# Block sums stored a group later, token blocks loaded a group sooner, and copied reciprocals in the attention

## The chip, the cores and the metric

One core of a Trainium2 chip runs the whole program. TensorE (PE) multiplies matrices, PEld is its weight load, VectorE (DVE), ScalarE (ACT) and GpSimd (POOL) work on tiles, and SyncE (SP) issues DMAs from one queue, in order. The metric is the device time of one execution in microseconds, as a median of runs. "Granted clock" is the share of TensorE's full clock that the throttle gave.

## What is computed

Attention between tokens and a small state for 8 batches, then eight experts of equal capacity, then a gated layer (silu) over all 4608 tokens:

```python
def reference(**kwargs):
    attn_out = _attn_ref(x, state)            # 8 batches, 8 heads, 512 tokens, 32 states, 64 wide
    x = attn_out.transpose(0, 2, 1, 3).reshape(B * S, H * D)   # 4608 x 512
    x = _moe_ref(x=x, **moe_kwargs)           # 8 experts of 576 tokens, 512 -> 1024 -> 512
    return _moe2_ref(x=x, **moe2_kwargs)      # 512 -> 1536 -> 512

def _moe2_ref(x, w_gate, w_val, w_out):
    g = x @ w_gate
    silu = g * (1.0 / (1.0 + np.exp(-g)))
    val = x @ w_val
    return (silu * val @ w_out).astype(np.float32)

def _attn_ref(x, state):
    scores = scale * np.matmul(x, state.transpose(0, 1, 3, 2))
    ...                                       # softmax over the states: a
    xread = np.matmul(a, state)
    scores2 = scale * np.matmul(state, x.transpose(0, 1, 3, 2))
    ...                                       # softmax over the tokens: a2
    sread = np.matmul(a2, x)
    return np.concatenate([xread, sread], axis=2).astype(np.float32)
```

## The kernel before

Four parts follow each other. The attention runs batch by batch up to some 150 us; the experts' tokens are then selected; eight experts run up to 649 us; the gated layer, here called the passes, fills the rest. In all of them a scheduler places the instructions on the engines' queues in list order, as far as the buffers of the tile pools allow; each engine then executes its own queue in order.

*Attention.* Float32 products are made from high and low halves: `turn_x` transposes tokens on PE, ACT casts the high half xTh (L235), DVE subtracts to get the low half xTl (L236). `prep_state` does the same for the state (SBh on ACT L198, SBl on DVE L199, four pieces of each). `scores` multiplies them into z (L249 to L251); `center` transposes z on DVE and subtracts the maximum on POOL (zc, L261). `xread` multiplies the exponentials e1h and e1l (e1l on POOL, L286) with the state into px, ACT copies px to xu (L321), DVE makes the reciprocals rd (L325, L326), weights the gate's columns with them (xw, L327), and POOL weights the values with the same rd (xm, L333). This happens twice in each batch, for two halves of its tokens.

*Passes.* The gated layer is a seven-product scheme in blocks. `hidden_units` lists two passes, of nine groups each (eight experts' tokens and the remainder group E in the middle), and of three units in each group; unit (n, jj) here is the jj-th of the n-th group of the first pass. A unit is 84 matmuls on PE (L1076) into four banks. ACT copies the first bank (s1, L1106), DVE adds the others up (u2 L1109, u3 L1112, cs L1115, L1121, L1124), ACT and DVE apply the gate (m, L1083 and L1084), and SP stores m (L1127). PE uses the banks of the unit before the last again, so it waits when s, u or cs are late.

Between a unit's steps the next group's operands are made: `y_load` (L955) loads a block of tokens, `y_sums` lets POOL form four sums of it (L902 to L905, tiles tt, a ring of six), `keep` stores them for the second pass (L878), and `y_combo` splits each operand into a high half (ACT, L864) and a low half (DVE, L865), in a ring of tiles yb. An operand comes straight from the loaded block (raw: 1, 2, 3) or from a sum (6, 7, 5, 4). Pairs of weight blocks go the same way (L890 to L893, w). `convert` turns a block of weights as loaded (raw64, one buffer, L171) into float32 with ACT (L179) and DVE (L181, L182, L184), and SP stores it (v_d, L185), and then loads the next block into that one buffer.

## Time and profile before

| | us |
|---|---|
| median of 3 runs | 1452.44 (1451.69 to 1453.4) |
| profiled execution | 1450.2 |
| its span | 1448.6 |
| PE busy in it | 1368.3 (94%) |
| DVE busy | 1072.4 (74%) |
| ACT busy | 571.5 (39%) |
| POOL busy | 455.8 (31%) |

The profiled execution is one run of its own, and all durations below are from it; 1.6 us of it lie outside the span. Busy shares are means over the four parts. Idle time of PE is put down to what ended it: the row of a matmul has it in brackets, with the engine and the tile that came last.

### The profile page before, as it was taken

How to read it: one execution, taken by the hardware profiler on the slowest of the kernel's cores; microseconds unless marked ns; L12 is line 12 of the kernel's file. 1: busy time of each engine (PE TensorE's matmuls, PEld its weight loads, DVE VectorE, ACT ScalarE, POOL GpSimd, SP SyncE). 2: the span in 40 equal slices, each digit the busy share in tenths (PEclk: the TensorE clock that was granted, in tenths of full speed). 3: DMA queues.
4: the chain of work that ended last, by engine and by line, in shares of the span. 5: the costliest groups of instructions: out<-in, count | busy, mean ns of one | idle time of the engine just before them, and what ended most of it. 6: DMA issues, size and time to landing. Idle time of an engine off the chain costs nothing.

```text
span 1448.6 us, 28968 instructions
## 1 busy us (share of the span) xinstructions
PE 1368.3 (94%) x11440; PEld 1323.6 (91%) x11441; DVE 1072.4 (74%) x2052; ACT 571.5 (39%) x1124; POOL 455.8 (31%) x392
## 2 busy tenths in 40 slices
PE   6998388999999999999999999999999999999996
PEld 5777278999999999999899999999999999999996
DVE  5899768876877765558776766777756588998982
ACT  6875123332333334345233333433323264444441
POOL 4775211100110110333442300112311007778872
PEclk9999699999999999999999999999999999999999
DMA  7542324444446355427674563766675384434431
GB/s 132 127 116 85 116 70 175 155 150 155 131 137 197 125 156 176 162 79 269 209 278 171 189 204 114 250 228 233 227 274 183 114 308 154 146 121 159 158 102 44
DMA packets 122823, 238.36 MB, mean 165 GB/s; under 512 B 47808, under 2 KB 57024, under 8 KB 116288
## 3 DMA queue, kind: packets, MB, share of 16 engines
q1 hardware_dynamic: 109008, 207.65, 42.8%
q0 software_dynamic: 6112, 19.93, 4.1%
q10 hardware_dynamic: 7568, 8.95, 2.0%
q8 instruction: 89, 1.46, 0.4%
q14 instruction: 46, 0.38, 0.1%
HBM read 153.65 MB, written 82.84 MB: 163 GB/s over the span
## 4 chain that ended last, share of the span: by engine, by line
PE 75%; issue 5%; DMA 3%; DVE 3%; ACT 1%; POOL 0%; SPq 0%; POOLq 0%; DVEq 0%; ACTq 0%
PE b L1076 47%; PE h L821 13%; PE y L840 4%; PE y L836 4%; PE y L837 4%; PE bt L800 1%; DVE yb L865 1%; DMA raw<-in_moe_w_val_dram 1%; DMA raw<-y_d 1%; DMA xg<-xm_d,idx 1%; DMA raw<-v_d 0%; DMA v_d<-tt 0%; PE acc L476 0%; PE acc L565 0%; DVE cs L1115 0%
## 5 line engine op out<-in xcount | busy, mean ns | idle before, releaser
L1076 PE MATMUL b<-yb,w 128*128 128x256 f32 x4320 | 519.7, 283 | 11.1 <-DVE cs L1115 6.9
L1076 PEld LDWEIGHTS b<-yb,w 128*128 128x128 f32 x4320 | 517.0, 191 | 13.6 <-DVE cs L1115 8.1
L1076 PE MATMUL b<-w,yb 128*128 128x256 f32 x2160 | 257.5, 282 | 0.0
L1076 PEld LDWEIGHTS b<-w,yb 128*128 128x128 f32 x2160 | 257.4, 189 | 0.0
L821 PE MATMUL h<-xh,w 128*128 128x288 f32 (+1 forms) x1024 | 212.0, 298 | 1.3 <-ACT xh L805 0.7
L865 DVE TENSOR_TENSOR yb<-tt,yb 128x512 fp32r<-128x512 f32 x164 | 153.4, 950 | 18.4 <-ACT yb L864 17.3
L821 PEld LDWEIGHTS h<-xh,w 128*128 128x128 f32 x1024 | 163.7, 191 | 3.2 <-DVE hl L826 1.1
L791 POOL DMA_INDIRECT xg<-xm_d,idx x38 | 47.9, 1260 | 370.2 <-PE bt L800 185.2
L890 POOL TENSOR_TENSOR tt<-raw 128x512 f32<-128x512 f32 (+1 forms) x33 | 44.0, 1336 | 338.5 <-DVE yb L865 102.2
L821 PE MATMUL h<-xl,w 128*128 128x288 f32 (+1 forms) x512 | 149.4, 294 | 0.1
L864 ACT CAST yb<-tt 128x512 fp32r<-128x512 f32 x164 | 100.5, 620 | 102.0 <-PE b L1076 75.5
L836 PE MATMUL y<-hh,w 128*128 128x288 f32 (+1 forms) x512 | 136.1, 292 | 3.5 <-ACT hh L825 3.5
L837 PE MATMUL y<-hh,w 128*128 128x288 f32 (+1 forms) x512 | 135.9, 292 | 0.5 <-DVE w L749 0.5
L865 DVE TENSOR_TENSOR yb<-raw,yb 128x512 fp32r<-128x512 f32 x127 | 125.0, 991 | 15.0 <-ACT yb L864 14.1
L825 ACT ACTIVATE hh<-h 128x288 fp32r<-128x288 f32 (+1 forms) x128 | 50.9, 397 | 194.0 <-PE h L821 176.9
L826 DVE SCALAR_TENSOR_TENSOR hl<-h,hh 128x288 fp32r<-128x288 f32 (+1 forms) x128 | 55.6, 435 | 66.9 <-ACT hh L825 66.1
L864 ACT CAST yb<-raw 128x512 fp32r<-128x512 f32 x127 | 78.0, 620 | 58.9 <-PE b L1076 52.1
L836 PEld LDWEIGHTS y<-hh,w 128*128 128x128 f32 x512 | 96.6, 189 | 4.0 <-ACT hh L825 3.8
L821 PEld LDWEIGHTS h<-xl,w 128*128 128x128 f32 x512 | 97.4, 191 | 0.6 <-DVE xl L806 0.3
L837 PEld LDWEIGHTS y<-hh,w 128*128 128x128 f32 x512 | 96.8, 189 | 0.8 <-DVE w L749 0.7
L840 PE MATMUL y<-hl,w 128*128 128x288 f32 (+1 forms) x512 | 90.7, 294 | 0.0
L749 DVE TENSOR_TENSOR w<-raw,w 128x1024 fp32r<-128x1024 f32 x60 | 72.7, 1238 | 16.7 <-ACT w L748 16.5
(258 smaller groups left out, 2012.5 us busy)
## 6 DMA issues: line engine op xcount, KB each, us to landing
raw<-in_moe_w_dram SPq DMA_DIRECT2D x60, 512.0 KB, 5.2
raw<-m_d SPq DMA_DIRECT2D x28, 1024.0 KB, 4.9
m_d<-m SPq DMA_DIRECT2D x48, 512.0 KB, 3.5
raw<-v_d SPq DMA_DIRECT2D x32, 512.0 KB, 4.5
raw<-y_d SPq DMA_DIRECT2D x14, 1024.0 KB, 5.1
xm_d<-xm SPq DMA_DIRECT2D x8, 1024.0 KB, 5.1
y_d<-ys SPq DMA_DIRECT2D x16, 512.0 KB, 6.3
sums_dy<-tt SPq DMA_DIRECT2D x32, 256.0 KB, 2.2
```

The costliest lines, as they stand in the source:

```text
L749: eng.tensor_tensor(lo, raw, f32(hi), OP.subtract)
L791: hooks["g"] = nc.gpsimd.indirect_dma_start(out=xg[:n], out_offset=None, in_=xm_d, in_offset=bass.IndirectOffsetOnAxis(ap=idx[i][:n, j:j + ...
L821: hooks["p"] = nc.tensor.matmul(ph, W[i][0][k][q == 1][:, fs], (xl if q == 2 else xh)[:, k, :T], start=(n == 0), stop=(n == 11)).ins
L825: relu[16 * i + 8 * hf + f] = hooks["hh"] = nc.scalar.activation(hh, ph, AF.Relu).ins
L826: hooks["h"] = nc.vector.scalar_tensor_tensor(hl, ph, 0.0, f32(hh), op0=OP.max, op1=OP.subtract).ins
L836: nc.tensor.matmul(p[d], wh[:, f % 2, ds_], hh, start=(f == 0), stop=False)
L837: nc.tensor.matmul(p[d], wl[:, f % 2, ds_], hh, start=False, stop=False)
L840: nc.tensor.matmul(p[d], wh[:, f % 2, ds_], hl, start=False, stop=(f == 7))
L864: nc.scalar.copy(hi, src)
L865: nc.vector.tensor_tensor(lo, src, f32(hi), OP.subtract)
L890: nc.gpsimd.tensor_tensor(S1, a21, a22, OP.add)
L1076: nc.tensor.matmul(p[:, q], a(x, q), b(y), skip_group_check=True, start=start and not (q or n or m), stop=stop and q == 1 and n == last an ...
```

## The change

In the attention, `prep_state` writes its four ACT copies first and its four DVE subtractions then, and for the first batch it stands ahead of the turns of the tokens. `xread` copies the reciprocals rd into a tile of their own, rm, on DVE, 15 times in all, and POOL's xm reads rm.

In the passes, `keep` no longer issues its stores at once; they are collected and issued behind the next unit (`flush`). A token block is loaded two groups ahead, at the last unit of a group, and its sums are made behind the first unit of the next. The operands that come straight from the block (1, 2, 3) are split ahead of those that come from sums (6, 7, 5, 4).

```diff
--- before.py
+++ after.py
@@ -196,6 +196,10 @@
                 p = slice(64 * h, 64 * h + 64)
                 c = slice(64 * k + 32 * h, 64 * k + 32 * h + 32)
                 nc.scalar.copy(sh[p, k::2, c], v[p, :, k, h, :])
+        for k in range(2):
+            for h in range(2):
+                p = slice(64 * h, 64 * h + 64)
+                c = slice(64 * k + 32 * h, 64 * k + 32 * h + 32)
                 nc.vector.tensor_tensor(sl_[p, k::2, c], v[p, :, k, h, :], f32(sh[p, k::2, c]), OP.subtract)
         sT = st.setdefault(b, {})["sT"] = aw.tile([64, 2, 128], F32, name="sT", bufs=1)
         nc.scalar.copy(sT, pt[:64, :256].rearrange("p (g c) -> p g c", g=2))
@@ -328,6 +332,11 @@
             if b == B - 1:
                 nc.vector.tensor_reduce(Lw[:, 4 * b + r - 1:4 * b + r + 1, :], xw[:, q].rearrange("p r h e -> p r e h"),
                                         AX.X, OP.add)
+
+            if b < B - 1 or r == 1:
+                rm = aw.tile([128, 2, H], F32, name="rm", bufs=2)
+                nc.vector.tensor_copy(rm, rd)
+                rd = rm
 
             def values(rd=rd):
                 hooks["m"] = nc.gpsimd.tensor_tensor(xm[:, q], xu[:, :, :, :D],
@@ -602,9 +611,9 @@
     IE = sel.tile([128, 129, 4], BF, name="IE")
 
 
+    prep_state(0)
     for r in range(4):
         turn_x(0, r)
-    prep_state(0)
     prep_gate(0)
 
     for b in range(B + 1):
@@ -872,10 +881,17 @@
 
     sums_d = {}
 
-    def keep(key, S):
+    kept_later = []
+
+    def flush():
+        while kept_later:
+            nc.sync.dma_start(*kept_later.pop(0))
+
+    def keep(key, S, pool):
         sums_d[key] = [dram.tile([128, 2, 256], F32, name=f"sums_d{key}{i}") for i in range(4)]
-        for d, t in zip(sums_d[key], S):
-            nc.sync.dma_start(d, t)
+        kept_later.extend(zip(sums_d[key], S))
+        if pool is bw:
+            flush()
 
     def kept(key, pool):
         S = [tmp(pool) for _ in range(4)]
@@ -904,7 +920,7 @@
             nc.gpsimd.tensor_tensor(T3, b22, b12, OP.subtract)
             nc.gpsimd.tensor_tensor(T4, T2, b21, OP.subtract)
             if key:
-                keep(key, T)
+                keep(key, T, pool)
         return {1: b11, 6: T2, 7: T3, 2: b21, 5: T1, 4: T4, 3: b22}
 
     WC, Y, WO = {}, {}, {}
@@ -930,7 +946,7 @@
         else:
             S1, S2, S3, S4 = S = s_sums(A, pool, cut)
             if key:
-                keep(key, S)
+                keep(key, S, pool)
         whole = lambda t: [c(t) for c in cut]
         return {1: [a[0] for a in A], 6: whole(S2), 7: whole(S3), 2: [a[1] for a in A],
                 5: whole(S1), 4: [a[3] for a in A], 3: whole(S4)}
@@ -1146,7 +1162,7 @@
             else:
                 S1, S2, S3, S4 = S = s_sums([(a11, a12, a21, a22)], cw, [lambda t: t])
                 if key:
-                    keep(key, S)
+                    keep(key, S, cw)
             return {1: a11, 6: S2, 7: S3, 2: a12, 5: S1, 4: a22, 3: S4}
         a1, a2 = raw[:, :, 0], raw[:, :, 1]
         t, neg = tmp(cw), tmp(cw)
@@ -1187,22 +1203,25 @@
     src = pair_sums(pair_load(2, cw), cw, "w2")
     for n in PORDER:
         pair_combo(2, n, src)
-    ysrc = wsrc = None
+    ysrc = None
+    order9 = [g for p in range(2) for g in groups[p]]
+    yraw = y_load(groups[0][1], cw)
     for p, n, gi, jj in hidden_units:
         nxt = groups[p][n + 1] if n < E else None
-        if jj == (p == n == 0) and nxt is not None:
-            ysrc = y_sums(nxt, y_load(nxt, cw), cw)
+        if jj == 0 and gi == E:
+            ysrc = y_sums(nxt, yraw, cw)
+        k = 9 * p + n
+        if jj == 2 and k + 2 < len(order9) and (k + 1) % 9 < 8:
+            yraw = y_load(order9[k + 2], cw)
 
         def after(step):
             if nxt is None or (gi == E) != (step < 3 and gi == E):
                 return
             if gi == E:
-                todo = {(0, 1): (0, 1), (0, 2): (1, 2), (1, 1): (2, 3), (1, 2): (3, 4), (2, 1): (4, 5), (2, 2): (5, 7)}
-                a, b = todo[jj, step]
-                todo = PORDER[a:b]
+                todo = {(0, 1): (1,), (0, 2): (2,), (1, 1): (3,), (1, 2): (6,), (2, 1): (7,), (2, 2): (5, 4)}[jj, step]
             else:
-                todo = {(1, 1): (1,), (1, 7): (6,), (1, 5): (7,), (2, 1): (5,), (2, 6): (2,), (2, 2): (4,),
-                        (2, 5): (3,)}.get((jj, step), ())
+                todo = {(1, 1): (1,), (1, 7): (2,), (1, 5): (3,), (2, 1): (6,), (2, 6): (7,), (2, 5): (5,),
+                        (2, 2): (4,)}.get((jj, step), ())
             for m in todo:
                 if m in ysrc:
                     y_combo((p, nxt), m, ysrc)
@@ -1210,6 +1229,9 @@
         if n == E and p == 0 and jj == 0:
             wraw = pair_load(3, cw)
         unit(key, 3 * p + jj, gi, after)
+        flush()
+        if jj == 0 and gi != E and nxt is not None:
+            ysrc = y_sums(nxt, yraw, cw)
         a = {1: 0, 3: 1, 4: 2, 6: 3}.get(n) if p else None
         if a is not None:
             if jj == 1:
@@ -1248,6 +1270,8 @@
             key = (p, nxt)
         elif jj == 2 and p == 0:
             key = (0, gi)
+
+    flush()
 
 
     scat = []
```

POOL in a steady batch of the attention, before (RBl is the low half of the state's rows):

```order
L217 TENSOR_TENSOR RBl_112<-SC,RBh_110 32x2x73 x4
L333 TENSOR_TENSOR xm<-xu,rd 128x1024
L261 TENSOR_TENSOR zc<-zt,m_805 128x512
L261 TENSOR_TENSOR zc<-zt,m_823 128x512
L286 TENSOR_TENSOR e1l<-zb,e1h 128x512
L333 TENSOR_TENSOR xm<-xu,rd 128x1024
L286 TENSOR_TENSOR e1l<-zb,e1h 128x512
```

POOL in the same batch of the changed kernel (L342 is the new line of xm, L265 of zc, L290 of e1l, L221 of RBl):

```order
L221 TENSOR_TENSOR RBl_112<-SC,RBh_110 32x2x73 x4
L342 TENSOR_TENSOR xm<-xu,rm 128x1024
L265 TENSOR_TENSOR zc<-zt,m_813 128x512
L265 TENSOR_TENSOR zc<-zt,m_831 128x512
L342 TENSOR_TENSOR xm<-xu,rm 128x1024
L290 TENSOR_TENSOR e1l<-zb,e1h 128x512 x2
```

xm of the second half now stands ahead of both e1l, and both zc stay where they are.

DVE in the same place of a batch, around the reciprocals of the first half, before (ss is the state's result, zb a transposed zc):

```order
L325 TENSOR_SCALAR rd<-xu 128x16
L282 STREAM_TRANSPOSE zb<-zc 128x512
L326 RECIPROCAL rd<-rd 128x16
L236 TENSOR_TENSOR xTl<-pt,xTh 128x4x128
L327 TENSOR_TENSOR xw<-xu,rd 128x128
L236 TENSOR_TENSOR xTl<-pt,xTh 128x4x128
L365 TENSOR_TENSOR ss<-ps,rd_903 32x128 x4
```

DVE there in the changed kernel (L330 is the new line of the reciprocal, L331 of xw, L338 the copy, L240 xTl):

```order
L330 RECIPROCAL rd<-rd 128x16
L370 RECIPROCAL rd_1121<-rd_1121 128x2
L331 TENSOR_TENSOR xw<-xu,rd 128x128
L338 COPY rm<-rd 128x16
L286 STREAM_TRANSPOSE zb<-zc 128x512
L240 TENSOR_TENSOR xTl<-pt,xTh 128x4x128 x2
L374 TENSOR_TENSOR ss<-ps,rd_913 32x128 x4
```

xw has come ahead of both xTl, and the copy rm stands behind xw; xm waits for that copy.

DVE in unit (0, 1) of the passes, where the next group's operands are split, before (L865 is the split):

```order
L1109 TENSOR_TENSOR u_9355<-b_9351,s_9354 128x512
L1112 TENSOR_TENSOR u_9356<-b_9352,u_9355 128x512
L1115 TENSOR_TENSOR cs<-b_9353,u_9356 128x2x256
L865 TENSOR_TENSOR yb<-raw,yb 128x512
L865 TENSOR_TENSOR yb<-tt,yb 128x512 x2
L1084 TENSOR_TENSOR m<-b_9350,m 128x256
L1121 TENSOR_TENSOR cs<-u_9356,b_9351 128x2x256
L1124 TENSOR_TENSOR cs<-b_9353,u_9355 128x2x256
L865 TENSOR_TENSOR yb<-tt,yb 128x512
L865 TENSOR_TENSOR yb<-raw,yb 128x512
L1084 TENSOR_TENSOR m<-cs,m 128x768
```

DVE in the same unit of the changed kernel (L1125 is u2, L1128 u3, L1131, L1137 and L1140 cs, L1100 m, L874 the split):

```order
L1125 TENSOR_TENSOR u_9381<-b_9377,s_9380 128x512
L874 TENSOR_TENSOR yb<-raw,yb 128x512
L1128 TENSOR_TENSOR u_9382<-b_9378,u_9381 128x512
L874 TENSOR_TENSOR yb<-raw,yb 128x512
L1131 TENSOR_TENSOR cs<-b_9379,u_9382 128x2x256
L874 TENSOR_TENSOR yb<-raw,yb 128x512
L1100 TENSOR_TENSOR m<-b_9376,m 128x256
L1137 TENSOR_TENSOR cs<-u_9382,b_9377 128x2x256
L874 TENSOR_TENSOR yb<-tt,yb 128x512
L1140 TENSOR_TENSOR cs<-b_9379,u_9381 128x2x256
L874 TENSOR_TENSOR yb<-tt,yb 128x512 x3
L1100 TENSOR_TENSOR m<-cs,m 128x768
```

The three splits of raw blocks now stand between u and cs, and those of sums behind the second m.

DVE from the end of unit (1, 1) into unit (1, 2), before (L181, L182 and L184 are the conversion's three steps):

```order
L1084 TENSOR_TENSOR m<-cs,m 128x768
L865 TENSOR_TENSOR yb<-raw,yb 128x512
L1109 TENSOR_TENSOR u_9840<-b_9836,s_9839 128x512
L865 TENSOR_TENSOR yb<-tt,yb 128x512
L1112 TENSOR_TENSOR u_9841<-b_9837,u_9840 128x512
L865 TENSOR_TENSOR yb<-tt,yb 128x512
L1115 TENSOR_TENSOR cs<-b_9838,u_9841 128x2x256
L865 TENSOR_TENSOR yb<-tt,yb 128x512
L181 TENSOR_SCALAR tt<-raw_10095 128x512
L1084 TENSOR_TENSOR m<-b_9835,m 128x256
L182 SCALAR_TENSOR_TENSOR tt<-tt 128x512
```

DVE at the same place in the changed kernel:

```order
L1100 TENSOR_TENSOR m<-cs,m 128x768
L181 TENSOR_SCALAR tt<-raw_10121 128x512
L874 TENSOR_TENSOR yb<-raw,yb 128x512
L1125 TENSOR_TENSOR u_9872<-b_9868,s_9871 128x512
L874 TENSOR_TENSOR yb<-raw,yb 128x512
L1128 TENSOR_TENSOR u_9873<-b_9869,u_9872 128x512
L874 TENSOR_TENSOR yb<-raw,yb 128x512
L1131 TENSOR_TENSOR cs<-b_9870,u_9873 128x2x256
L874 TENSOR_TENSOR yb<-tt,yb 128x512
L182 SCALAR_TENSOR_TENSOR tt<-tt 128x512
```

L181 of the conversion stood behind cs (L1115), and now stands ahead of the unit's first u (L1125).

SP's queue at the same time, from the store of unit (1, 0) on, before (sums_dy are stores of sums, v_d of a converted block):

```order
L1127 DMA m_d_9185<-m 128x1024
L955 DMA raw<-yt_d 128x1024
L878 DMA sums_dy_9976<-tt 128x512
L878 DMA sums_dy_9977<-tt 128x512
L878 DMA sums_dy_9978<-tt 128x512
L878 DMA sums_dy_9979<-tt 128x512
L185 DMA v_d_1_166<-tt 128x512
L171 DMA raw_10095<-in_moe_w_val_dram 128x2x512
L1127 DMA m_d_9185<-m 128x1024
L919 DMA raw<-v_d_0_165 128x1024
```

SP from the same store on in the changed kernel (L888 is the store of sums, L971 the load of a token block):

```order
L1143 DMA m_d_9215<-m 128x1024
L888 DMA sums_dy_10110<-tt 128x512
L888 DMA sums_dy_10111<-tt 128x512
L888 DMA sums_dy_10112<-tt 128x512
L888 DMA sums_dy_10113<-tt 128x512
L185 DMA v_d_1_166<-tt 128x512
L171 DMA raw_10121<-in_moe_w_val_dram 128x2x512
L971 DMA raw<-yt_d 128x1024
L1143 DMA m_d_9215<-m 128x1024
L935 DMA raw<-v_d_0_165 128x1024
```

The four stores of sums_dy stay ahead of the v_d store and of the load of the next raw block; only yt_d's load has moved behind them.

SP just ahead of these rows, from the store of unit (0, 2) on, before:

```order
L1127 DMA m_d_9184<-m 128x1024
L878 DMA sums_dw_9958<-tt 128x512
L878 DMA sums_dw_9959<-tt 128x512
L878 DMA sums_dw_9960<-tt 128x512
L185 DMA v_d_0_165<-tt 128x512
L171 DMA raw_9829<-in_moe_w_val_dram 128x2x512
L878 DMA sums_dw_9961<-tt 128x512
L955 DMA raw<-y_d_64 128x2048
```

SP around the same store in the changed kernel:

```order
L888 DMA sums_dy_9734<-tt 128x512
L935 DMA raw<-v_d_1_163 128x1024
L971 DMA raw<-y_d_64 128x2048
L1143 DMA m_d_9214<-m 128x1024
L185 DMA v_d_0_165<-tt 128x512
L171 DMA raw_9859<-in_moe_w_val_dram 128x2x512
```

Before, the load of y_d_64, from which the sums sums_dy are made, stands behind that store, four stores of sums and a conversion's store and load; now it stands ahead of them.

## Rows read from the trace of the kernel before

**Rows 1.** Busy time by stretch: us; PE, PEld, DVE, ACT, POOL (instructions); granted clock; DMA; GB/s

```profile
50.00:75.00 25.00, 23.52 (x144) 20.11 (x143) 23.17 (x53) 21.13 (x60) 17.51 (x18) 1.00 0.58 133
675.00:700.00 25.00, 21.98 (x165) 21.37 (x166) 23.57 (x32) 7.80 (x14) 12.43 (x8) 0.93 0.65 218
700.00:725.00 25.00, 21.75 (x180) 21.34 (x179) 19.05 (x27) 8.35 (x15) 8.09 (x5) 1.00 0.62 214
750.00:775.00 25.00, 22.88 (x191) 22.68 (x191) 18.12 (x27) 6.95 (x12) 5.37 (x4) 1.00 0.57 200
680.00:685.00 5.00, 3.96 (x20) 3.96 (x21) 5.00 (x10) 2.33 (x5) 1.27 (x1) 0.66 0.90 329
725.00:730.00 5.00, 5.00 (x32) 5.00 (x32) 2.23 (x5) 0.73 (x2) 0.00 (x0) 0.66 0.97 311
```

**Rows 2.** The page's costliest groups: the passes' matmuls, idle time ahead, its releaser

```profile
L1076 PE MATMUL b<-yb,w 128*128 128x256 f32 x4320 | 519.7, 283 | 11.1 <-DVE cs L1115 6.9
```

**Rows 3.** Timeline (start, us, engine, line, operation), xw of three batches

```profile
37.65 1.85 DVE L327 TENSOR_TENSOR xw<-xu,rd 128x128 f32<-128x128 f32 x1
...
69.69 1.93 POOL L333 TENSOR_TENSOR xm<-xu,rd 128x1024 f32<-128x1024 f32 x1
69.84 1.92 DVE L327 TENSOR_TENSOR xw<-xu,rd 128x128 f32<-128x128 f32 x1
...
130.47 2.00 DVE L327 TENSOR_TENSOR xw<-xu,rd 128x128 f32<-128x128 f32 x1
```

**Rows 4.** By line: number of L327, L325, L326, shortest, median, longest in ns

```profile
L327 DVE TENSOR_TENSOR xw<-xu,rd x16: 273/292/2000, 37.7 to 147.5; 128x128 f32<-128x128 f32 x16
...
L325 DVE TENSOR_SCALAR rd<-xu x16: 155/342/1230, 36.3 to 146.1; 128x16 f32<-128x16 f32 x16
...
L326 DVE RECIPROCAL rd<-rd x16: 208/241/253, 36.9 to 147.1; 128x16 f32<-128x16 f32 x16
```

**Rows 5.** By line L236 (xTl): who waited for it, us and times

```profile
  PE z L250: 3.4, 5
...
  PE pt L232: 2.9, 2
```

**Rows 6.** Timeline, the first scores of the attention

```profile
13.34 0.50 PE L249 MATMUL z<-xTh,SBh 128*128 128x512 f32 x1 [1.34 <-ACT SBh L198]
```

**Rows 7.** Timeline, the second and third unit of the passes

```profile
665.37 1.30 POOL L902 TENSOR_TENSOR tt<-raw 128x512 f32<-128x512 f32 x1 [20.75 <-DMA raw<-y_d]
...
668.72 3.26 DVE L865 TENSOR_TENSOR yb<-tt,yb 128x512 fp32r<-128x512 f32 x2
...
674.30 0.57 ACT L1106 COPY s<-b 128x512 f32<-128x512 f32 x1
...
676.60 0.68 DVE L1109 TENSOR_TENSOR u<-b,s 128x512 f32<-128x512 f32 x1
...
677.33 1.69 PE L1076 MATMUL b<-yb,w 128*128 128x256 f32 x12 [0.74 <-DVE u L1109]
...
681.04 11.81 PE L1076 MATMUL b<-yb,w 128*128 128x256 f32 x84 [2.02 <-DVE cs L1115]
```

**Rows 8.** Timeline, units (1, 1) to (3, 0) of the passes

```profile
704.55 1.81 POOL L902 TENSOR_TENSOR tt<-raw 128x512 f32<-128x512 f32 x1 [7.54 <-DVE tt L182]
...
706.39 5.37 SPq L878 DMA_DIRECT2D sums_dy<-tt  x4
...
710.18 0.68 DVE L1109 TENSOR_TENSOR u<-b,s 128x512 f32<-128x512 f32 x1
...
712.33 0.41 SPq L171 DMA_DIRECT2D raw<-in_moe_w_val_dram  x1
...
717.14 0.68 ACT L179 ACTIVATE tt<-raw 128x512 f32<-128x512 f32 x1 [6.77 <-DMA raw<-in_moe_w_val_dram]
...
724.13 34.26 PE L1076 MATMUL b<-yb,w 128*128 128x256 f32 x276 [2.17 <-ACT s L1106]
...
760.51 9.73 PE L1076 MATMUL b<-yb,w 128*128 128x256 f32 x79 [2.12 <-DVE cs L1115]
```

## The prediction

> **What bounds the kernel now.** I read the busy time by stretch first. In the passes PE is full: outside three stretches of 25 us it is busy all the time or nearly so, and the whole idle time ahead of the passes' matmuls is 11.1 us [rows 2]. The three stretches are 675 to 700 (21.98 busy, so 3.02 idle), 700 to 725 (21.75, 3.25 idle) and 750 to 775 (22.88, 2.12 idle) [rows 1]: 8.4 of the 11.1 us. The stretch of 5 us at the first long gap, 680 to 685, has a granted clock of 0.66: part of it ran at 1.2 GHz instead of 2.4 [rows 1]; 725 to 730, behind the second, has the same 0.66. Each costs up to 5 x 0.34 = 1.7 us. The third long gap (2.12) is followed by no such fall. So the passes hold at most 11.1 + 3.4 = 14.5 us to win, and everything else in them is matmul time that the change leaves alone.
>
> In the attention (up to 150 us) PE is busy 23.52 and DVE 23.17 of 25 us, POOL 17.51 [rows 1]. No engine has much air, so a gain there needs work taken off DVE at a place for which PE waits. That place is in the timeline: POOL's xm (L333) starts at 69.69 and takes 1.93; DVE's xw (L327), a multiplication that reads the same xu and rd, starts 0.15 us later and takes 1.92, to the end of xm [rows 3]. Over all 16 xw the median is 292 ns and the longest 2000 [rows 4]; seven of the sixteen are long, the first at 37.65 and the last at 130.47 [rows 3], one in a batch, each starting some 0.15 us behind an xm. They stand ahead of the last xTl (L236) of the batch, and PE waits for xTl 3.4 us before z and 2.9 us before pt [rows 5].
>
> **The change part by part.**
>
> *State ahead of the tokens, four copies ahead of four subtractions.* The first z starts at 13.34 having waited 1.34 us for SBh [rows 6]. With all SBh copies in one row on ACT, ahead of the casts of the first turns, that wait goes; what is late next is xTh, cast from the transposes just ahead. I take -1.0 us; bounds 0 and -1.34. In the other batches ACT and DVE interleave these pieces with other work, so I count nothing there.
>
> *rd copied to rm; xm reads rm.* xm now can't start before xw is over, since the copy stands behind xw on DVE. Removed: seven long xw become short, 7 x (1.92 - 0.29) = 11.4 us of DVE. Added: 15 copies of 128x16. The nearest row is the reciprocal of the same shape, 241 ns (208 to 253) [rows 4]: 15 x 0.24 = 3.6 us. Far upper end: the tensor_scalar of that shape (L325) has 155 to 1230 ns for the same shape [rows 4]. All 15 at 1.23 would be 18.5 us, and DVE would lose 7.1 instead of winning 7.8. I take the reciprocal, since the copy stands right behind xw, where POOL waits for it. On the path counts what PE waits for: 3.4 + 2.9 = 6.3 us behind xTl at most. POOL gives some back: xm starts about 0.29 + 0.24 = 0.53 us later, and in the new order of POOL both e1l stand behind xm, where before one stood ahead; px on PE waits for e1l. I take -4.0 from the attention's batches; the bounds are -7.8 (all that DVE wins) and +7.1 (all that it would lose with held copies).
>
> The Trainium skill, "SBUF — State Buffer", section "Who interferes with whom", says that DVE copies and tensor_scalar operations between SBUF operands can take a port pair shared with GpSimd, and that whoever comes second waits whole. The xw that ends with xm, and the spread of L325, agree with it, and it speaks against this edit, since the copy is such an operation itself; by it the copies would tend to the upper end whenever POOL is at work, and the sum would lose the 4.0 us (the second rival below).
>
> *Raw blocks ahead of sums, sums one unit after the load (first gap pair).* From 665.37 on POOL computes the y sums [rows 7]. DVE has two yb<-tt ahead of m and of the two last cs, and that pair takes from 668.72 to 671.98 [rows 7]: behind it m, cs and then s, u are late. PE waits 0.74 at 677.33 for u and 2.02 at 681.04 for cs [rows 7]. In the new order of DVE the unit runs u, raw, u, raw, cs, raw, m, cs and only then the tt. The raw splits wait for the load alone, so u and cs no longer stand behind POOL. Price of each split is unchanged (0.68 alone, 1.2 to 1.8 beside POOL). Gain: 0.74 + 2.02 + 0.26 of the stretch, and the 1.7 of the clock: -4.7. I take -4.5.
>
> *Stores one unit later, loads sooner (second gap).* SP holds four stores of y3's sums from 706.39 to 711.8, since POOL is still making them [rows 8]. Behind them in SP's queue stand the store of the converted block and the load of the next raw block, issued at 712.33; ACT's conversion waits for it 6.77 us until 717.14 [rows 8]. Casts, cs, m and s behind it are late, and PE waits 2.17 at 724.13 [rows 8], with 1.7 of clock behind it. In the new order the four stores still stand ahead of that block's store and load, but y3's block is loaded a unit sooner. POOL began its sums at 704.55 after 7.54 us idle [rows 8]; with the block there it can begin up to 7.5 us sooner, as far as tt buffers are free, and I take 6, so the load would be issued near 706. Gain 2.17 + 1.7 = 3.9, and half of the 1.08 left in this stretch: -4.4. What is held longer: the tt tiles of the sums keep their six buffers until the later stores have landed, so POOL's next sums (behind L902 in its queue) start later; there is no row for this, the bounds are 0 and the 2.03 us of one sum operation held.
>
> *Third gap.* 2.12 at 760.51 [rows 8] comes from L182 ahead of cs, blocked beside POOL's sums. The order there stays, but loads come sooner: half, -1.1.
>
> Against this stand new waits: conversions (L181) now stand ahead of u or cs in some units. I count +1.5 (bounds 0 and +8). Passes: -4.5 - 4.4 - 1.1 + 1.5 = **-8.5** (bounds -13 and -1). Together with the attention, -1.0 - 4.0 - 8.5 = **-13.5**. The profiled run took 1450.2 with a span of 1448.6; so 1436.7 there. The median of the runs shown is 1452.4, 2.2 us above; on it the forecast is 1438.9, **1439 us**.
>
> **The rivals.**
> - *The passes' stalls only move.* The order of SP still has the sums' stores ahead of the raw load. For it: POOL's order is untouched, and PE's gaps follow chains of several hops. Against it: the first gap is cured by DVE's own order. The attention's -5 stay and about -2 of the passes: **1445**.
> - *The attention gives nothing.* POOL's e1l behind xm, or held copies, take the place of xTl. For it: DVE's L325 of up to 1.23 [rows 4]. Against it: xw is seven times plainly 1.92. Then -0.5 - 8.5: **1443**.
> - *Slower: L181 at the head of a unit.* In the new order of DVE unit (1, 2) begins with L181, ahead of u; two later units do too. If its raw block is issued as late as before (712.33) it lands at 717.14, against 710.18 for the unit's first u [rows 8]: u is held 7.0 us. From the first gap: s ended at 674.87, u began at 676.60, 1.73 later, and PE stood 0.74 [rows 7], so some 1.0 is slack. PE would stand 6.0, with 1.7 of clock 7.7 us; three times, 23. Against the 13.5 won that is +9.6: **1462**. It decides where the block lands more than 1 us behind the unit's head, and the sum turns slower at the second such unit. Against it: the load should be issued near 706 and land near 711, 4.8 later, within the slack of the head.
> - *The change doesn't do what it says.* Work waits for buffers as before, everything keeps its times: **1452**.
>
> **How the numbers follow.** (A measurement of this kernel tells about 0.2%, 2.9 us, from no change.) Chances: forecast 0.54, stalls only move 0.15, attention gives nothing 0.13, slower 0.08, no change 0.10. The range runs from 1430 (attention -9, of its bounds, and passes -13: -22) to 1451 (copies held at +7 with the passes' -8.5: -1.4); below and above it I leave 2 in 10. Faster by more than 0.2% is below 1449.5: forecast and first two rivals, 0.82, less 0.02 of their upper tails: 0.80. Same: 0.11. Slower: 0.09.
>
> **What would show it.** In the profile after, all xw (L327 before) take near 0.29, and the copies 0.1 to 0.3; copies of 1 us refute the second step. PE's wait for xTl falls from 6.3 to under 3; waits for e1l would show POOL in its place. The stretches 675 to 700, 700 to 725 and 750 to 775 (all some 5 us sooner) should have PE busy above 24.5 with a granted clock of 1.00. A DVE wait for the raw block before L181 with u behind it and PE idle over 2 us shows the slower rival. The forecast is wrong above all if new gaps open in other units of the passes, which were full.

## The result, and the profile after

The changed kernel took 1462.74 us (median of 4 runs, 1462.16 to 1465.18) against 1452.92 for the kernel before (1451.69 to 1454.41): a ratio of 1.0082, with a 95% interval of 1.0064 to 1.0101. It is 0.8% slower, where I had forecast 0.9% faster and a range up to 1451. Its profiled run took 1463.3, with a span of 1461.7.

The two halves of the change went different ways. The passes begin at 644.80 instead of 649.50, so the attention gave 4.7 us (5.0 were forecast). From there to the end the kernel took 1461.7 - 644.8 = 816.9 us, where it had taken 1448.6 - 649.5 = 799.1: the passes lost 17.8 us, where a gain of 8.5 was forecast. First the page's costliest group in the profile after, which answers to [rows 2] (name, count, busy and mean, then idle time ahead and what ended most of it):

```profile
L1092 PE MATMUL b<-yb,w 128*128 128x256 f32 x4320 | 524.1, 284 | 24.5 <-DVE cs L1131 18.6
```

The idle time ahead of the passes' matmuls went from 11.1 to 24.5 us, and 18.6 of it now ends with cs on DVE. That is 13.4 of the 17.8 us; the other 4.4 are in the group's busy time, 519.7 before and 524.1 now for the same 4320 matmuls. The stretches show where (columns as in [rows 1]):

```profile
50.00:75.00 25.00, 24.50 (x150) 20.73 (x149) 21.28 (x61) 22.34 (x65) 18.13 (x20) 1.00 0.73 173
675.00:700.00 25.00, 23.05 (x188) 22.65 (x189) 21.72 (x32) 5.67 (x10) 13.09 (x9) 1.00 0.82 288
700.00:725.00 25.00, 25.00 (x214) 25.00 (x213) 19.68 (x31) 9.94 (x17) 6.32 (x5) 1.00 0.59 199
750.00:775.00 25.00, 23.59 (x197) 23.38 (x196) 17.01 (x27) 8.29 (x15) 4.03 (x4) 1.00 0.51 178
...
830.00:855.00 25.00, 18.85 (x145) 18.65 (x145) 12.85 (x21) 6.46 (x11) 0.00 (x0) 0.86 0.52 169
1110.00:1135.00 25.00, 20.07 (x149) 19.87 (x148) 13.81 (x22) 8.72 (x16) 1.05 (x1) 0.86 0.56 184
835.00:840.00 5.00, 2.44 (x11) 2.44 (x12) 3.42 (x6) 0.26 (x1) 0.00 (x0) 0.50 0.54 170
```

The three stretches that I had watched all became better: 21.98, 21.75 and 22.88 us of PE before, 23.05, 25.00 and 23.59 now, all at a clock of 1.00; but my sign was above 24.5, and only the second reached it. Two stretches of which I had said nothing lost 6.15 and 4.93 us, and in the five microseconds from 835 the granted clock is 0.50, which is 1.2 GHz throughout; PE had stood still from 831.4 to 837.6. Here is the first of the two in the timeline (start, duration, engine, line and operation, in brackets the idle time ahead and what ended it):

```profile
822.92 5.54 SPq L888 DMA_DIRECT2D sums_dy<-tt  x4
...
828.56 0.87 SPq L935 DMA_DIRECT2D raw<-v_d  x2
...
834.36 0.62 ACT L873 CAST w<-raw 128x512 fp32r<-128x512 f32 x1 [8.48 <-DMA raw<-v_d]
...
835.01 0.69 DVE L874 TENSOR_TENSOR w<-raw,w 128x512 fp32r<-128x512 f32 x1 [4.88 <-ACT w L873]
...
835.62 0.68 DVE L1128 TENSOR_TENSOR u<-b,u 128x512 f32<-128x512 f32 x1
...
836.82 0.68 DVE L1131 TENSOR_TENSOR cs<-b,u 128x512 f32<-128x512 f32 x1
...
837.56 4.70 PE L1092 MATMUL b<-yb,w 128*128 128x256 f32 x24 [6.15 <-DVE cs L1131]
```

SP holds the four stores of sums_dy for 5.54 us, since POOL is still making the sums; behind them in its queue stands the load of a pair of weight blocks (raw<-v_d), issued at 828.56. ACT's cast w<-raw waits 8.48 us for it. On DVE the split w<-raw (L874) waits for that cast, and behind it in DVE's queue stand u3 (L1128) and cs (L1131), for which PE waits 6.15 us. The same load in the kernel before:

```profile
827.83 5.59 SPq L878 DMA_DIRECT2D sums_dy<-tt  x4
...
833.52 0.88 SPq L919 DMA_DIRECT2D raw<-v_d  x2
...
836.07 0.68 DVE L1112 TENSOR_TENSOR u<-b,u 128x512 f32<-128x512 f32 x1
...
836.86 0.69 DVE L1115 TENSOR_TENSOR cs<-b,u 128x512 f32<-128x512 f32 x1
...
839.52 0.62 ACT L864 CAST w<-raw 128x512 fp32r<-128x512 f32 x1 [7.35 <-DMA raw<-v_d]
...
840.18 0.69 DVE L865 TENSOR_TENSOR w<-raw,w 128x512 fp32r<-128x512 f32 x1 [2.63 <-ACT w L864]
```

It was held as long (5.59 us) and came as late, but u3 and cs stood ahead of the split, and PE did not stop for them. Only the place in DVE's queue is new, and it stands in the order itself. Unit (6, 0) on DVE in the kernel before:

```
L1109 TENSOR_TENSOR u_11297<-b_11293,s_11296 128x512
L182 SCALAR_TENSOR_TENSOR tt<-tt 128x512
L184 SCALAR_TENSOR_TENSOR tt<-raw_11643,tt 128x512
L1112 TENSOR_TENSOR u_11298<-b_11294,u_11297 128x512
L1115 TENSOR_TENSOR cs<-b_11295,u_11298 128x2x256
L865 TENSOR_TENSOR w<-raw,w 128x512
```

and in the changed kernel:

```
L1125 TENSOR_TENSOR u_11311<-b_11307,s_11310 128x512
L182 SCALAR_TENSOR_TENSOR tt<-tt 128x512
L874 TENSOR_TENSOR w<-raw,w 128x512
L1128 TENSOR_TENSOR u_11312<-b_11308,u_11311 128x512
L184 SCALAR_TENSOR_TENSOR tt<-raw_11675,tt 128x512
L1131 TENSOR_TENSOR cs<-b_11309,u_11312 128x2x256
```

These weights are needed only for the last group of the pass. As I read the program, three tiles of their ring (24, of which three pairs hold 21) are free, so the scheduler hoists the first splits by two groups to wherever its plan has a hole; no run tests this reading by itself. The second long gap is the same thing in unit (6, 1) of the second pass, with cs alone behind the split:

```profile
1104.67 6.73 SPq L888 DMA_DIRECT2D sums_do<-tt  x3
...
1111.49 0.88 SPq L1181 DMA_DIRECT2D raw<-v_d  x2
...
1117.44 0.62 ACT L873 CAST w<-raw 128x512 fp32r<-128x512 f32 x1 [9.45 <-DMA raw<-v_d]
...
1118.09 0.69 DVE L874 TENSOR_TENSOR w<-raw,w 128x512 fp32r<-128x512 f32 x1 [7.17 <-ACT w L873]
...
1118.70 0.68 DVE L1131 TENSOR_TENSOR cs<-b,u 128x512 f32<-128x512 f32 x1
...
1119.44 4.85 PE L1092 MATMUL b<-yb,w 128*128 128x256 f32 x21 [4.93 <-DVE cs L1131]
```

A third gap is ACT's. In unit (2, 1) the conversion's first step (L179) now stands ahead of the gate and of the next unit's s, and waits 9.15 us for a tile of the ring tt that a store of sums still reads:

```profile
735.90 0.66 ACT L179 ACTIVATE tt<-raw 128x512 f32<-128x512 f32 x1 [9.15 <-DMA sums_dw<-tt]
...
736.47 0.83 ACT L1099 ACTIVATE m<-cs 128x768 f32<-128x768 f32 x1
...
737.20 0.57 ACT L1122 COPY s<-b 128x512 f32<-128x512 f32 x1
...
737.82 14.87 PE L1092 MATMUL b<-yb,w 128*128 128x256 f32 x108 [3.02 <-ACT s L1122]
```

It is not the only one of its kind. In three other places the conversion's step on DVE (L181) waits for a ring tile that a store of sums still reads: 1.90 us ahead of a gap of 1.30 at 697.59, 3.53 ahead of 1.96 at 949.84 and 0.47 right behind it, and 2.69 ahead of 0.89 and 1.05 near 1005. The four places together are 8.7 us of idle PE, beside the 11.1 us of the weights' splits.

### The profile page after: what moved, and what is told of

Read it like the earlier page. It is cut to its first block, busy times and chain, and to the rows that moved or that the text cites. A ratio compares the mean times of both kernels' runs of the same rounds, so it can differ in the third digit from the quotient of the medians.

```text
span 1461.7 us, 28972 instructions
## 1 busy us (share of the span) xinstructions
PE 1374.3 (94%) x11441; PEld 1327.8 (91%) x11441; DVE 1058.4 (72%) x2067; ACT 570.6 (39%) x1124; POOL 450.1 (31%) x392
## 4 chain that ended last, share of the span: by engine, by line
PE 67%; DMA 7%; DVE 6%; issue 3%; POOL 2%; ACT 1%; SPq 0%; POOLq 0%; DVEq 0%; ACTq 0%
PE b L1092 38%; PE h L830 13%; PE y L849 4%; PE y L846 4%; PE y L845 4%; DVE yb L874 1%; PE bt L809 1%; DMA raw<-y_d 1%; DMA raw<-in_moe_w_val_dram 1%; DMA sums_da<-tt 1%; DMA sums_dw<-tt 1%; DVE m L1100 1%; DMA raw<-v_d 1%; DVE w L758 1%; PE acc L485 0%
## 5 line engine op out<-in xcount | busy, mean ns | idle before, releaser
L1092 PE MATMUL b<-yb,w 128*128 128x256 f32 x4320 | 524.1, 284 | 24.5 <-DVE cs L1131 18.6
L874 DVE TENSOR_TENSOR yb<-tt,yb 128x512 fp32r<-128x512 f32 x164 | 152.1, 942 | 14.9 <-ACT yb L873 13.5
L874 DVE TENSOR_TENSOR yb<-raw,yb 128x512 fp32r<-128x512 f32 x127 | 124.5, 988 | 14.7 <-ACT yb L873 14.0
```

What stands on the lines that cost most here:

```text
L874: nc.vector.tensor_tensor(lo, src, f32(hi), OP.subtract)
L1092: nc.tensor.matmul(p[:, q], a(x, q), b(y), skip_group_check=True, start=start and not (q or n or m), stop=stop and q == 1 and n == last an ...
```

## Which edits lost it

Every run below is compared with runs of the kernel before on the same chip; "gap" is idle time of PE in the passes. Two theories stood against each other: (A) the new order of the splits lets the scheduler put a weight's split ahead of u3 and cs; (B) the loads and the later stores make the gaps, since they hold ring tiles and SP's queue.

**The attention's edits alone** (the diff's first three parts on the kernel before):

```diff
+        for k in range(2):
+            for h in range(2):
...
+                rm = aw.tile([128, 2, H], F32, name="rm", bufs=2)
+                nc.vector.tensor_copy(rm, rd)
...
+    prep_state(0)
```

> The attention's edits alone (the state's copies ahead of its subtractions, the copied reciprocals), with the passes of before. In the changed kernel the passes begin at 644.80 instead of 649.50. Theory: this 4.7 us is all the attention's, so 1452.9 - 4.7 = 1448 us, and the passes take 799 us as before. Rival: the earlier start shifts the scheduler's and the DMAs' timing in the passes and gives the gain back, 1451 or more.

Measured: 1447.49 us, ratio 0.9964 (0.9950 to 0.9978). The attention's part is a gain of 4.4 us, and it stays where the passes are as before (1443.2 - 643.7 = 799.5 us from their start).

**The passes' edits alone** (the other parts on the kernel before):

```diff
+            yraw = y_load(order9[k + 2], cw)
...
+        flush()
```

> The passes' edits alone, with the attention of before. Theory: they lose 17.8 us, most of it in two places (PE idle 6.15 us near 837 and 4.93 us near 1119, with the clock that follows), and do so whatever the attention does: 1467 to 1471 us. Rival: the loss hangs on how the attention's end shifts the passes, then below 1460.

Measured: 1468.66 us, ratio 1.0117 (1.0089 to 1.0146). The long gaps are there at 840.59 (6.24 us) and 1123.85 (4.20), and one of 4.01 at 741.26. The loss belongs to the passes' edits, whatever the attention does.

**The changed kernel with the old order of the splits** (for the remainder group E too, which is not shown):

```diff
...
-                todo = {(1, 1): (1,), (1, 7): (2,), (1, 5): (3,), (2, 1): (6,), (2, 6): (7,), (2, 5): (5,),
-                        (2, 2): (4,)}.get((jj, step), ())
+                todo = {(1, 1): (1,), (1, 7): (6,), (1, 5): (7,), (2, 1): (5,), (2, 6): (2,), (2, 2): (4,),
+                        (2, 5): (3,)}.get((jj, step), ())
```

> The changed kernel with the old order of the operands' splits (1, 6, 7, 5, 2, 4, 3 instead of raw blocks first). Theory A: the new order of the splits is what let the scheduler put a weight's split (w<-raw) ahead of u3 in unit (6, 0) and ahead of cs in unit (6, 1) of the second pass; with the old order both stand behind cs, the two long gaps go (11 us, and some 4 us of clock) and the time is 1447 to 1449 us. Theory B: the loads and the later stores make the gaps, the time stays at 1458 or more. The gap of 3.0 us near 738 stays by both, if the later stores make it.

Measured: 1456.00 us, ratio 1.0026 (1.0010 to 1.0042). Both theories miss. The gaps here are those of its profiled run, which took 1460.59 us, 4.6 above the median. The gap near 837 is gone (0.72 left), but others opened: 3.26 at 1000.09, 3.83 at 1123.39, and 3.82 at 738.79 stayed. The one at 1123 is a weight's split again:

```profile
1105.06 7.90 SPq L888 DMA_DIRECT2D sums_do<-tt  x3
...
1120.05 0.62 ACT L873 CAST w<-raw 128x512 fp32r<-128x512 f32 x1 [8.67 <-DMA raw<-v_d]
...
1120.70 0.69 DVE L874 TENSOR_TENSOR w<-raw,w 128x512 fp32r<-128x512 f32 x1 [7.57 <-ACT w L873]
...
1121.31 0.68 DVE L1140 TENSOR_TENSOR cs<-b,u 128x512 f32<-128x512 f32 x1
...
1123.39 1.86 PE L1092 MATMUL b<-yb,w 128*128 128x256 f32 x7 [3.83 <-ACT s L1122]
```

In its order the split stands ahead of the third cs (L1140), as in the kernel before, and the stores hold SP for 7.90 us, so the third cs, the gate and s are late. The old order of the splits avoids the worst place and not the cause.

**Only the new order of the splits, on the kernel before** (again with group E, not shown):

```diff
...
-                todo = {(1, 1): (1,), (1, 7): (6,), (1, 5): (7,), (2, 1): (5,), (2, 6): (2,), (2, 2): (4,),
-                        (2, 5): (3,)}.get((jj, step), ())
+                todo = {(1, 1): (1,), (1, 7): (2,), (1, 5): (3,), (2, 1): (6,), (2, 6): (7,), (2, 5): (5,),
+                        (2, 2): (4,)}.get((jj, step), ())
```

> Before with the new order of the splits alone (stores and loads as before). Theory A: the two long gaps are there, and the first long gaps (2.8 us near 680) go: 1452.9 + 15 - 4 = 1464 us. Theory B: 1452 or less.

Measured: 1459.73 us, ratio 1.0053 (1.0037 to 1.0069). Its two long gaps are 5.95 us at 840.71 and 4.17 at 1116.17. So the order alone makes both; but it did not close the first gaps (0.73 and 2.30 near 680), so my reading of those was wrong too. It did close the second pair (1.08 at 714.61 and 2.17 at 724.13 before), with loads and stores as they were, and opened one of 2.25 at 704.79.

**The changed kernel with stores at once:**

```diff
-        if pool is bw:
-            flush()
+        flush()
```

> The changed kernel with the sums' stores issued at once again, as before; loads and order of the splits stay new. Its order on VectorE still has w<-raw ahead of u3 and of cs at the two places. Theory: the later stores hold tiles of the ring tt for which the conversion's first steps (L179 on ScalarE, L181 on VectorE) wait, which makes the gap of 3.0 us near 738 and part of the 5.1 us between 950 and 1017; these go and the two long gaps stay: 1453 to 1457 us. Rival: later stores cost nothing, the order does it all: 1460 or more.

Measured: 1464.55 us, ratio 1.0077 (1.0048 to 1.0106), all three gaps there (3.09, 8.29 and 6.17). Taken back alone, the later stores cost nothing that can be seen.

**The changed kernel with loads and sums as before:**

```diff
+        if jj == (p == n == 0) and nxt is not None:
+            ysrc = y_sums(nxt, y_load(nxt, cw), cw)
...
```

> The changed kernel with token blocks loaded one group ahead and sums made ahead of the unit, as before; later stores and the new order of splits stay. Theory: the early loads are what closes the gaps near 681, 715 and 724, so these come back: 1464 to 1468 us. Rival: loads sooner only take ring tiles and SP's queue sooner and are part of the loss: 1458 or less.

Measured: 1467.04 us, ratio 1.0109 (1.0084 to 1.0134). The two gaps stay (6.34, 6.23). The 2.30 at 675.67 is back, and 2.54 at 700.01 stands where the changed kernel has 1.30 and the kernel before had none; the gaps near 715 and 724 do not come back. The intervals of e8 and of the changed kernel overlap, so what the early loads are worth is seen only in these two places: 2.30 against 1.42 us and 2.54 against 1.30.

**What loads and stores cost together.** Each taken back alone wins nothing, but both together do. With loads and stores of before, the new order costs 0.5% (e4, 1.0053); with the new ones it costs 1.2% (e2, 1.0117). With the old order, the new loads and stores cost the difference of e3 to e1, 1.0026 to 0.9964. Both pairs say some 9 us, beside the 8 us of the order alone, and the two add up to about what the passes lost. What differs is in the traces: the conversion's L179 in unit (2, 1) waits 9.15 to 10.15 us for a store of sums in the changed kernel, e2, e3, e5 and e8, and in e4 it runs at 740.36, behind the gate and s, without a wait. So theory B was half of the answer: beside the new order, early loads or later stores are enough, each by itself, to bring these gaps.

**The weights' splits queued behind a gate.** The constraint adds no wait between engines; it only fixes the order on two queues:

```diff
...
+            ga, gd = hooks[0, 6, 0]
+            with tc.issue_after(ga), tc.issue_after(gd):
                 for m in PORDER:
                     pair_combo(3 + jj, m, src)
...
```

(and the same for the second pass behind unit (6, 1); `hooks` holds the gate's two instructions of each unit.)

> The changed kernel with one constraint more: the splits of the weights w that are made ahead of the last group of a pass are queued behind the gate of unit (6, 0), in the second pass (6, 1), on VectorE and ScalarE. Nothing else is asked for. Theory: the two gaps of 6.15 and 4.93 us and some 4 us of clock go, 1447 to 1450 us. Rival: the weight's block lands so late that the split stalls the next unit as long: 1458 or more.

Measured: 1450.08 us, ratio 0.9996 (0.9979 to 1.0014): 12.7 us less than the changed kernel, 12.5 by the ratios. The page's group and the place of the first gap:

```profile
L1092 PE MATMUL b<-yb,w 128*128 128x256 f32 x4320 | 522.8, 284 | 14.1 <-DVE cs L1131 8.9
```

```profile
826.33 0.88 SPq L935 DMA_DIRECT2D raw<-v_d  x2
...
829.03 0.68 DVE L1131 TENSOR_TENSOR cs<-b,u 128x512 f32<-128x512 f32 x1
...
829.76 10.26 PE L1092 MATMUL b<-yb,w 128*128 128x256 f32 x84 [0.56 <-DVE cs L1131]
...
833.48 0.62 ACT L873 CAST w<-raw 128x512 fp32r<-128x512 f32 x1
...
834.13 0.69 DVE L874 TENSOR_TENSOR w<-raw,w 128x512 fp32r<-128x512 f32 x1
...
840.12 0.69 DVE L874 TENSOR_TENSOR w<-tt,w 128x512 fp32r<-128x512 f32 x1 [4.70 <-ACT w L873]
...
842.26 5.95 PE L1092 MATMUL b<-yb,w 128*128 128x256 f32 x35 [2.24 <-DVE cs L1131]
```

The load is as late as ever (826.33), cs now goes at 829.03 and PE waits 0.56 instead of 6.15; at the other place, in the second pass, PE runs on without a gap. That one place in a queue, twice, is most of the loss. The constraint only reaches unit (6, 0), though: in the next unit the second split of the same pair (w<-tt), for which a stored sum is loaded, stands ahead of u3 again and costs 2.24 us.

**Both e6 and stores at once:**

```diff
-        if pool is bw:
-            flush()
+        flush()
...
+            ga, gd = hooks[0, 6, 0]
+            with tc.issue_after(ga), tc.issue_after(gd):
```

> The constraint of e6 and the stores at once of e5 together; early loads, new order of the splits and the attention's edits stay. Theory: the two causes add up, 1438 to 1444 us, faster than before by some 0.8%. Rival: they are the same cause seen twice, then no better than the better of the two.

Measured: 1451.15 us, ratio 0.9997 (0.9984 to 1.0010). Nothing is added by it, in line with e5.

## What the remaining gaps are made of

e6 is no faster than before although its attention is: 14.1 us of idle time are left, 3.15 of them at the conversion on ACT. I moved that conversion alone:

```diff
...
+            if V == 8:
+                with tc.issue_after(hooks[0, 2, 1][0]):
+                    convert(16 + CT.index(V), cw)
```

> e6 with one constraint more: the conversion that stood ahead of the gate on ScalarE in unit (2, 1) (L179, behind which m and s wait, PE idle 3.15 us at 736.47 in e6) is queued behind that gate. Theory: that gap and its clock go, 1450.1 - 3.2 - 1.7 = 1445 us, as far as the following conversions, which move with it, open no new gaps. Rival: the tile it waits for is the matter, and the gap moves to the next unit: 1449 to 1451.

Measured: 1454.97 us, ratio 1.0030 (1.0012 to 1.0049), slower than e6. In its profiled run (1461.03 us, 6.1 above the median) the gap at 736 is gone, 2.41 at 759.98 and 2.28 at 777.17 are new, and the 2.24 of e6 has become 3.55 at 849.04. Only at 777.17 is it a conversion that slid into the middle of a unit (L181, which waits 2.83 us for its block ahead of the last cs); at 759.98 an operand's split waits 5.39 us on DVE, by way of ACT's cast, for POOL's sums, and at 849.04 it is the weight's second split. I then put all conversions between units:

```diff
-            convert(16 + CT.index(V), cw)
+            ga, gd = hooks[p, n, jj]
+            with tc.issue_after(ga), tc.issue_after(gd):
+                convert(16 + CT.index(V), cw)
```

> e6 with every conversion of the passes queued behind the gate of the unit after which the program writes it, on ScalarE and VectorE, so that each stands between two units and none between u, cs and m of one that has the block's load to wait for. The weights' splits go back behind the conversions, three units later. Theory: what is left in the passes is made by conversions that the scheduler puts ahead of u and cs; idle falls from 14 us to under 6 and the time to 1437 to 1442. Rival: the splits of the token blocks and POOL's sums are what delays u and cs, then 1447 or more.

Measured: 1442.22 us, ratio 0.9929 (0.9901 to 0.9956). The time came as the theory said, just at its end, but 10.5 us of idle time are left where it had under 6. Then the same constraint, with the diff just shown, on e1 (the attention's edits and the passes of before), on the kernel before alone, and on the changed kernel without a constraint on the weights:

> e1 (the attention's edits alone) with the same constraint on the conversions, and the passes else as before. Theory: with the conversions between the units the passes of before lose their gaps (10.9 us idle, 3.4 clock) as well, by half at least: 1447.5 - 7 = 1440 us, near e10, so that early loads, later stores and the new order of splits are worth little. Rival: these edits are needed for the gain, then e11 stays at 1446 or more while e10 is faster.

Measured: 1437.94 us, ratio 0.9913 (0.9891 to 0.9936).

> Before with nothing but the constraint on the conversions (each queued behind the gate of the unit after which the program writes it). e11 had it with the attention's edits: 1437.9 us, of which the attention is 4.4. Theory: the conversions' places alone are worth 9 to 10 us, 1442 us. Rival: they need the attention's shift, 1446 or more.

Measured: 1443.28 us, ratio 0.9935 (0.9912 to 0.9957).

> The changed kernel with the constraint on the conversions and none on the weights' splits. In its order the weights' splits go back by three units by themselves. Theory: the conversions' places decide where the scheduler puts the weights' splits, so both long gaps go without a constraint of their own: 1440 to 1444 us, as e10. Rival: the splits of the weights need their own constraint, then a gap over 3 us shows and the time is 1447 or more.

Measured: 1440.17 us, ratio 0.9922 (0.9901 to 0.9942). The pages' groups of e14 and e15:

```profile
L1076 PE MATMUL b<-yb,w 128*128 128x256 f32 x4320 | 518.5, 283 | 6.2 <-DVE cs L1115 4.6
```

```profile
L1092 PE MATMUL b<-yb,w 128*128 128x256 f32 x4320 | 516.6, 282 | 7.9 <-ACT s L1122 4.6
```

One rule on the conversions' place takes the idle time of the kernel before from 11.1 to 6.2 us and that of the changed one from 24.5 to 7.9, and in both the weights' splits go back by three or four units by themselves. So one constraint on the conversions is enough to take away most of both kinds of gap. That a conversion holds DVE or ACT between u and cs until its block has landed, or a ring tile is free, is in the rows above; that it pushes what is planned around it is my explanation, which no run tests by itself. The constraint does two things at once, it moves them between units and spaces them by two units, and these runs don't tell the one from the other. With them between the units, the passes' three edits make no difference that these runs can tell (e15 against e11: 0.9922 and 0.9913, with intervals of 0.002 to either side).

## Which of the attention's edits

The copies alone, on the kernel before:

```diff
+            if b < B - 1 or r == 1:
+                rm = aw.tile([128, 2, H], F32, name="rm", bufs=2)
+                nc.vector.tensor_copy(rm, rd)
+                rd = rm
```

> Before with the copied reciprocals alone. Theory: the seven long xw end, 3.4 to 4 us of the 4.4 that the attention's edits gave in e1 are theirs, 1448 us. Rival: the state's copies ahead of the subtractions give most of it, 1451 or more.

Measured: 1450.84 us, ratio 0.9997 (0.9983 to 1.0011): nothing that can be told. The copies do what I said, and the gain does not come; by line, the copies (L334), xm (L338) with the engine's idle time before it, and PE's wait behind xTl:

```profile
L334 DVE COPY rm<-rd x15: 159/167/473, 38.7 to 145.7; 128x16 f32<-128x16 f32 x15
```

```profile
L338 POOL TENSOR_TENSOR xm<-xu,rm x15: 1915/1920/1927, 38.9 to 146.0; 128x1024 f32<-128x1024 f32 x15
...
  DVE rm L334: 9.6, 4
```

```profile
  PE pt L232: 2.9, 2
```

The copies take 167 ns, the wait of z for xTl (3.4 us in [rows 5]) is gone, but POOL now stands 9.6 us for the copies, and pt's 2.9 us are still there. Then the state's part alone:

```diff
+    prep_state(0)
     for r in range(4):
         turn_x(0, r)
-    prep_state(0)
...
+        for k in range(2):
+            for h in range(2):
+                p = slice(64 * h, 64 * h + 64)
+                c = slice(64 * k + 32 * h, 64 * k + 32 * h + 32)
```

> Before with the state's part alone: four copies ahead of four subtractions, and the first batch's state ahead of its tokens. e1 (both parts of the attention) gave 4.4 us, e12 (the copies alone) 0.9. Theory: the two parts add up, and this one gives 3 to 4 us, 1448 to 1449 us, mostly in the batches behind the first, where PE's wait for pt behind xTl (2.9 us in two waits, still there in e12) goes. Rival: only both together give it, since the shorter xw is used up by what the state's pieces wait for; then this one stays at 1451 or more.

Measured: 1441.36 us, ratio 0.9938 (0.9920 to 0.9955): 10.8 us, more than both edits together (e1). The state's pieces in a steady batch before:

```profile
59.12 0.21 ACT L198 CAST SBh<-pt 64x64 fp32r<-64x64 f32 x1 [0.38 <-PE pt L192]
...
59.77 0.21 DVE L199 TENSOR_TENSOR SBl<-pt,SBh 64x64 fp32r<-64x64 f32 x1
...
60.97 0.21 ACT L198 CAST SBh<-pt 64x64 fp32r<-64x64 f32 x1
...
61.73 0.23 DVE L199 TENSOR_TENSOR SBl<-pt,SBh 64x64 fp32r<-64x64 f32 x1
...
61.99 0.21 ACT L198 CAST SBh<-pt 64x64 fp32r<-64x64 f32 x1
...
62.70 0.22 DVE L199 TENSOR_TENSOR SBl<-pt,SBh 64x64 fp32r<-64x64 f32 x1
...
63.46 0.21 ACT L198 CAST SBh<-pt 64x64 fp32r<-64x64 f32 x1
```

and in e13:

```profile
57.16 0.87 ACT L198 CAST SBh<-pt 64x64 fp32r<-64x64 f32 x4
...
58.06 0.22 DVE L203 TENSOR_TENSOR SBl<-pt,SBh 64x64 fp32r<-64x64 f32 x1 [0.34 <-ACT SBh L198]
...
59.85 0.23 DVE L203 TENSOR_TENSOR SBl<-pt,SBh 64x64 fp32r<-64x64 f32 x1
```

Before, the four casts on ACT are spread over 59.12 to 63.67, one behind each subtraction on DVE; in e13 they take 0.87 us in one piece. Counted from the batch's sum over xw (L343 before, at 60.21, and at 59.22 in e13), the last subtraction ends 3.7 us behind it before and 0.9 us behind it in e13. The batch's period falls from 15.0 us (60.21 to 75.18) to 14.0 (59.22 to 73.18), though the longest xw still takes 2.0 us, and the passes begin 7.0 us sooner, at 642.47; another 1.8 us of this profiled run lie in the passes (797.3 us in the place of 799.1), which the edit does not name. Which of the edit's two places gave the gain was not run apart, but the first batch did not start sooner: its first xw runs at 38.3, and at 37.65 before. Last, e13 with the constraint on the conversions (the diff of e10), and e15 without the copies:

> Before with the state's copies ahead of its subtractions (e13: 10.8 us) and the constraint on the conversions (e14: 8.9 us), without the copied reciprocals and without the passes' edits. Theory: attention and passes add up, 1452 - 10.8 - 8.9 = 1432 to 1434 us, faster than e11 (1437.9), which has the copied reciprocals too. Rival: the copies are needed once the state is first, then 1437 or more.

Measured: 1436.61 us, ratio 0.9888 (0.9867 to 0.9909).

```diff
-            if b < B - 1 or r == 1:
-                rm = aw.tile([128, 2, H], F32, name="rm", bufs=2)
-                nc.vector.tensor_copy(rm, rd)
-                rd = rm
```

> e15 (the changed kernel with the constraint on the conversions, 1440.2 us) without the copied reciprocals. Theory: the copies cost what e1 is slower than e13, some 6 us, so 1434 to 1436 us, near e16: the passes' edits are worth nothing once the conversions stand well. Rival: 1440 or more, and the copies cost nothing here.

Measured: 1435.56 us, ratio 0.9879 (0.9857 to 0.9901). These two are the fastest, 1.1 to 1.2% below the kernel before, and can't be told apart. That the copies cost something beside the state's new order is likely (e13 against e1, e17 against e15), but e16 against e11 shows only 0.9888 to 0.9913 with overlapping intervals; how much they cost stays open.

## Point by point

- **The attention, -5.0: right in size, by luck.** 4.7 us were won. The step "in the other batches I count nothing there" was the one that failed: it is the state's new order that gave the gain (e13), not the copies, which I had put at -4.0 (e12: 0.9 us, not told from zero). The sign that I had named for the copies came all the same: PE's wait behind xTl fell from 6.3 to 1.1 us in the changed kernel, and no xw takes more than 1.13. A wait that ends is not yet time won. The start's -1.0 did not come: the first z runs at 13.45, against 13.34 in [rows 6]. The last xTh is now cast at 12.57 instead of 11.61, which I had named as late next and not priced, and PE has the gate's products (L213) ahead of z, from 12.46 to 13.5. The price of a copy was good: 163 ns by the median in the profile after, against my 240; the longest of the 15 took 1.25 us. The Trainium skill ("SBUF — State Buffer", "Who interferes with whom") has the copy take a port pair for which it may wait for GpSimd; the longest copy, which began 0.09 us behind an e1l on POOL and ended with it, and xw's 1.9 us beside xm, agree with it, and the copies' median shows that this edit seldom meets it.
- **The first gap pair, -4.5: about half.** PE waits 0.79 at 664.18, one unit sooner, and 1.42 at 675.43 in the place of 0.74 and 2.02 in [rows 7], and the clock stays at 1.00: some 2.3 us. e4 shows that the order of the splits alone closes nothing there, e8 that the early loads do part of it.
- **The second gap, -4.4: right in size.** The stretch from 700 to 725 is full. The raw block's load went out at 698.57, sooner than the 706 of my sum, and L181 at the head of unit (1, 2) waited 0.67 us. But the edit to which I gave this is not the only one that does it: in e4, with loads and stores of before, the load goes out at 705.77 and both waits are gone too. **The third, -1.1:** 0.7 us.
- **New waits, +1.5: the step that failed.** They came to 1.3 + 3.0 + 6.2 + 5.1 (five between 949 and 1007) + 4.9 = 20.5 us (the kernel before had 2.4 in their places), with their clock still to add, against +1.5 in my sum and a bound of 8. Of these, 11.1 are the two splits of weights, which the prediction does not have at all, and 8.7 the conversions that wait for a ring tile; I had put the tiles that are held longer at 2.03 us at most, and only for POOL's next sums. I had read the new order only where the old gaps were, and had written that everything else in the passes is matmul time that the change leaves alone. The order on DVE of unit (6, 0), shown above, was there to be read.
- **The rival for the slower side** gave 1462 us by one instruction that waits for a load at the head of a DVE queue, with u behind it. Its mechanism was the right one, but its instruction and its places were wrong, and that its time came out is luck: of the three units that begin with L181, that of unit (1, 2) waited 0.67 us and one at 959.34 waited 0.74, and both cost nothing, the third waited 2.69 (for a ring tile, not its block) and made gaps of 0.89 and 1.05 us near 1005, and the large part came from the split of a weight in two other units. I gave it 0.08.

## What to carry to other kernels

Where a scheduler sets the order, an edit of one loop moves instructions that the edit does not name. Before a time is forecast, go through every unit of the new order, not only those with a gap today: for each engine on the chain, what newly stands ahead of the chain's instructions, and which transfer does that wait for. And where work that is not urgent (a conversion, an operand needed later) may be hoisted into the middle of an urgent chain, one constraint of order that keeps it between the units can be worth more than loading sooner: here it took 9 us off the kernel before, alone.

## What was not expected of the hardware

The clock falls unevenly. The five microseconds in which PE starts again behind the gap of 6.15 us (835 to 840) have a granted clock of 0.50, those with the gap of 2.02 us in the kernel before 0.66 (680 to 685), and with one of 2.12 (760 to 765) it stays at 1.00. Of the 17.8 us that the passes lost, 4.4 are in the matmuls' own busy time and 13.4 in gaps, so on average a gap cost about a third more than it shows. The 4.4 us are the clock's, by an estimate: a matmul takes 0.112 us in stretches of 5 us at 1.00, and in the stretches below 1.00 (two before, eight after) the matmuls counted there took 3.1 us longer than that before, and 7.4 after.
